# A state-space layer with a gated FFN: parameters turned on VectorE, full-height products first, loads reordered

## The chip, the cores and the metric

The kernel runs on one core of a Trainium2 chip. The time is device microseconds of one launch, the median over several runs; lower is better. Engines: TensorE (PE, matrix products; its weight loads are listed as PEld), VectorE (DVE), ScalarE (ACT), GpSimd (POOL), SyncE (SP, which here only issues DMAs). SP, ACT and POOL each have a queue from which DMAs are issued (SPq, ACTq). "span" is the time from the first to the last instruction in the profile.

## The reference

The input is one sequence of 2048 tokens with 512 features, in bf16. It is normalised, and two branches are multiplied and added to the input:

```python
xn = _layernorm(x, axis=-1)                       # x: 1 x 2048 x 512
s  = _A_ref(xn, ...)                              # linear recurrence over tokens
g  = _silu(_B_ref(xn, w_gate, w_up, w_down))      # gated FFN
return x + s * g

# _A_ref: P = 512 complex states
dt = exp(log_dt);  Lam = Lambda_re + 1j * Lambda_im
Lam_bar = exp(dt * Lam)
B_bar = ((Lam_bar - 1) / Lam)[:, None] * (B_re + 1j * B_im)
Bu = x @ B_bar.T
h[t] = Lam_bar * h[t-1] + Bu[t]
y = 2 * (h @ C.T).real + x * Dskip
# _B_ref: F = 1376
(gelu(x @ w_gate) * (x @ w_up)) @ w_down
```

## The kernel before

The 2048 tokens are cut into NS = 4 stripes of 512 tokens, each of M = 4 tiles of 128 tokens. A stripe goes through these stages:

- **Normalise**: `stats` (VectorE, mean and variance of a tile), `rstd` (VectorE adds epsilon into `ve`, GpSimd raises it to the power -0.5 into `rs`), `norm_dve` (VectorE writes the normalised tile `xn`).
- **Transpose** the tile to `xnT`, features on the partitions. In stripe 0 this is `head_t`: four TensorE transposes into a PSUM bank and a ScalarE eviction (L404). Later stripes use a DMA transpose.
- **Gate and up products** (`gate_pair` in stripe 0, `gate_tile` later): xnT times w_gate and w_up, whose 1376 columns are cut into the chunks `CH` = 512, 512, 352. A ScalarE gelu evicts the one (`gt`), a ScalarE copy the other (`ub`), and VectorE multiplies the two into `at`. Stripe 0 does the first chunk for all four tiles, then the second for all four, then the recurrence's input products, then the last chunk.
- **Recurrence** (`half`): products with B (`BT`), a rotation by tables of sines and cosines (`tab`, made once by `tables` from the angle dt times Lambda_im), a VectorE scan with the real decay `rho` (made by `damping`), and the rotation back into `hst`.
- **Down products** (`down_pair`) with w_down, silu, and **output** (`y_tile`): products of `hst` with C, times silu, plus x, stored.

PSUM holds three double banks (`slots`) and two single ones (`ybank`). A gate chunk of one tile takes one slot; the fourth tile of the first chunk takes the two ybanks. A slot is free for its next products when both evictions are done.

Nothing here runs in the order of the source text. Each piece of work is a step that is added to a plan (class `Plan`) with an engine, a cost in us, what it reads and writes, a lag, and a `rank` that raises its priority. The plan orders the steps on each engine with a list scheduler and a random search over its own modelled times, and emits them in the order of these modelled starts. TensorE's steps alone are chained in the order in which they were added. On the chip each engine works through its own list strictly in order. `not_before` is the earliest modelled start; `after` and `dma_first` chain the first DMAs of a queue.

What the change touches stands at the head of the program:

- `dummies(8, 0)` (L393): eight products of 128x512 on a tile of ones (`warm`, the same memory as `junk`), with which TensorE is kept busy until the first tile arrives. The name `slot<-junk` is theirs.
- `load_p`: three parameter vectors of 512 values (`log_dt`, `Lambda_im`, `Lambda_re`), loaded as four rows of 128 into `pv`.
- `columns` (L674, called by `parameters` and `damping`): turns such rows into columns of four values on 128 partitions, by TensorE products with a 4x4 identity (4 rows of contraction), and a VectorE copy (L676) into `pf`. Before them, exp of log_dt (L356) and the product with Lambda_im (L358) are formed on the rows.
- `spread` (L690): one product with one row of contraction, which broadcasts Dskip to all partitions.
- the two one-element activations at L355 and L357, which bring the exp and the sine table into ScalarE; the third table, gelu, comes with L459.
- the order of the first loads on SP, ACT and POOL.

The order on TensorE before is: dummies, transposes of tile 0, `parameters` (five instructions at L674), one more dummy, gate products of tile 0 (L453), `spread`, transposes of tile 1, up products of tile 0, transposes of tile 2, and so on; `damping`'s product with Lambda_re comes after the second tile.

## Time and profile before

| what | value |
|---|---|
| median of 6 runs | 182.38 us (181.33 to 183.39) |
| the six runs | 183.39, 183.26, 183.27, 181.33, 181.33, 181.49 |
| the profiled execution | 183.39 us, span 181.6 us |
| TensorE busy | 176.3 us, 97% of the span |
| VectorE, ScalarE, GpSimd busy | 157.7, 117.7, 9.7 us |
| granted TensorE clock in the records | 1.00 |
| moved by DMA | 18.01 MB, 99 GB/s on average |

The table is read so: the busy shares are sums over the whole span, and a matrix product counts as busy from its start to its modelled end, overlapping its successor. The time of a launch is longer than the span of the profile by what lies around the first and the last instruction, 1.79 us in the profiled execution. The lines of the profile that carry the argument are shown with the prediction. Line numbers such as L453 are those of the kernel before.

### The profile page before, as it was taken

Reading aid. Unit: us, or ns where it says so; the run is one execution under the profiler, and the core shown is the slowest. Engines: PE = TensorE matmul, PEld = TensorE weight load, DVE = VectorE, ACT = ScalarE, POOL = GpSimd, SP = SyncE. Lnnn points to the kernel's source line nnn. Section 1 sums busy time; section 2 is a strip of 40 time slices with the busy share of each in tenths; the row PEclk is TensorE's granted clock in tenths of the full one; section 3 lists DMA queues with packets and bytes.
Section 4 is the critical chain, followed back from the end, with each engine's and each line's share of the span. In section 5 each row is a group of like instructions: output and inputs, shape, how many; then the busy total and the mean of one; then the engine's idle time right before and its main releaser. Section 6 shows DMA issues by size and latency. Waiting matters only on the chain.

```text
span 181.6 us, 2419 instructions
## 1 busy us (share of the span) xinstructions
PE 176.3 (97%) x856; PEld 84.2 (46%) x856; DVE 157.7 (87%) x267; ACT 117.7 (65%) x179; POOL 9.7 (5%) x21
## 2 busy tenths in 40 slices
PE   6999999999999999999999999999999999999992
PEld 2444444644445554444445544544445554444451
DVE  4859999999999999899999999999999999750063
ACT  5279688899899996866339953726428766454220
POOL 5410220000003000000020000000000000000000
PEclk9999999999999999999999999999999999999999
DMA  5999999995000178440021651451000070720011
GB/s 130 370 304 236 360 116 184 280 210 111 0 0 0 22 145 111 80 79 0 0 87 34 125 115 35 79 110 32 29 0 29 12 142 21 150 85 29 0 58 58
DMA packets 47139, 18.01 MB, mean 99 GB/s; under 512 B 38456, under 2 KB 47128, under 8 KB 47128
## 3 DMA queue, kind: packets, MB, share of 16 engines
q1 hardware_dynamic: 46544, 17.34, 42.3%
q10 hardware_dynamic: 552, 0.53, 1.1%
q8 instruction: 6, 0.10, 0.2%
q14 instruction: 5, 0.04, 0.1%
q0 software_dynamic: 32, 0.00, 0.0%
HBM read 6.33 MB, written 2.10 MB: 46 GB/s over the span
## 4 chain that ended last, share of the span: by engine, by line
PE 96%; DVE 2%; issue 0%; DVEq 0%
PE slot L474 31%; PE slot L517 21%; PE slot L585 15%; PE ybank L547 14%; PE slot L453 10%; PE slot L393 2%; PE ybank L453 1%; PE ybank L401 1%; DVE yg L551 1%; DVE ot L559 1%; PE slot L674 1%; PE slot L690 0%; DVE junk L348 0%; DVE at L352 0%; PE ybank L674 0%
## 5 line engine op out<-in xcount | busy, mean ns | idle before, releaser
L474 PEld LDWEIGHTS <-xnT 128*128 128x128 bf16 x288 | 28.2, 98 | 28.4
L517 PE MATMUL slot<-wd,atT 128*128 128x512 bf16 (+1 forms) x176 | 38.7, 379 | 0.0
L474 PE MATMUL slot<-wu,xnT 128*128 128x512 bf16 (+1 forms) x144 | 31.8, 357 | 0.0
L474 PE MATMUL slot<-wg,xnT 128*128 128x512 bf16 (+1 forms) x144 | 31.8, 357 | 0.0
L618 DVE TENSOR_TENSOR_SCAN Fs<-rho,ini,W 128x512 bf16<-128x512 f32 x24 | 29.2, 1265 | 0.0
L585 PE MATMUL slot<-xnT,BT 128*128 128x512 bf16 x128 | 28.3, 379 | 0.0
L547 PE MATMUL ybank<-C,hst 128*128 128x512 bf16 (+1 forms) x128 | 27.9, 372 | 0.0
L517 PEld LDWEIGHTS <-atT 128*128 128x128 bf16 (+1 forms) x176 | 17.2, 98 | 20.9
L588 ACT ACTIVATE U<-slot 128x1024 bf16<-128x1024 f32 x16 | 16.1, 1019 | 9.2 <-PE slot L585 9.2
L551 DVE TENSOR_TENSOR yg<-ybank,g 128x512 bf16<-128x512 f32 (+1 forms) x14 | 9.4, 669 | 13.7 <-PE ybank L547 13.6
L547 PEld LDWEIGHTS <-hst 128*128 128x128 bf16 x136 | 13.3, 98 | 13.8
L585 PEld LDWEIGHTS <-BT 128*128 128x128 bf16 x128 | 12.5, 98 | 15.0
L599 DVE TENSOR_TENSOR Q<-U,tab 128x4096 bf16<-128x4096 bf16 x8 | 18.3, 2289 | 0.6 <-ACT U L588 0.3
L521 ACT ACTIVATE g<-slot 128x1024 f32<-128x1024 f32 x8 | 8.2, 1023 | 16.3 <-PE slot L517 16.3
L599 DVE TENSOR_TENSOR Q<-Fs,tab 128x4096 bf16<-128x4096 bf16 x8 | 18.3, 2285 | 0.1
L543 ACT ACTIVATE ybank<-sk 128x512 f32<-128x512 bf16 (+1 forms) x14 | 8.2, 585 | 12.8 <-DVE yg L551 11.1
L482 ACT ACTIVATE gt<-slot 128x1024 bf16<-128x1024 f32 x12 | 12.3, 1023 | 4.3 <-PE slot L474 4.2
L482 ACT ACTIVATE ub<-slot 128x1024 bf16<-128x1024 f32 x12 | 12.3, 1023 | 3.4 <-PE slot L474 3.2
L453 PEld LDWEIGHTS <-xnT 128*128 128x128 bf16 x96 | 9.6, 101 | 9.3 <-issue 1.4
L453 PE MATMUL slot<-wg,xnT 128*128 128x512 bf16 (+1 forms) x44 | 11.1, 378 | 0.0
L453 PE MATMUL slot<-wu,xnT 128*128 128x512 bf16 (+1 forms) x44 | 10.7, 366 | 0.0
L776 ACT ACTIVATE junk<-x_tok 128x512 bf16<-128x512 bf16 x16 | 10.0, 627 | 0.3
(120 smaller groups left out, 181.9 us busy)
## 6 DMA issues: line engine op xcount, KB each, us to landing
out_dram<-ot SPq DMA_DIRECT2D x15, 128.0 KB, 1.7
x_tok<-in_A_x_dram SPq DMA_DIRECT2D x3, 512.0 KB, 8.1
wd<-in_B_w_down_dram SPq DMA_DIRECT2D x1, 1280.0 KB
wu<-in_B_w_up_dram SPq DMA_DIRECT2D x2, 512.0 KB, 5.6
x_tok<-in_A_x_dram SPq DMA_DIRECT2D x4, 128.0 KB, 4.1
wg<-in_B_w_gate_dram ACTq DMA_DIRECT2D x1, 512.0 KB, 4.5
wg<-in_B_w_gate_dram SPq DMA_DIRECT2D x1, 512.0 KB
wg<-in_B_w_gate_dram SPq DMA_DIRECT2D x1, 352.0 KB, 4.3
```

Source lines behind the costliest of these rows:

```text
L453: T.matmul(pss[bank][:, 0:w], lhsT=xnT[:, k, t0 : t0 + P], rhs=wt[:, k, a:b], start=(k == 0), stop=(k == KT - 1))
L474: T.matmul(ps[:, bank, 0 : b - a], lhsT=xnT[:, k, t0 : t0 + P], rhs=wt[:, k, a:b], start=(k == 0), stop=(k == KT - 1))
L482: acts(1024, lambda ps=ps, dst=dst, fn=fn: act(out=dst[:, 0:1024].rearrange("p (c w) -> p c w", c=2), in_=ps[:, :, :], func=fn), [("slot", ...
L517: T.matmul(ps[:, b, :], lhsT=atT[:fs, k, m * P : (m + 1) * P], rhs=wd[:fs, k, :], start=(k == 0), stop=(k == NFT - 1))
L521: acts(1024, lambda: act(out=g2[gi][:, :, :], in_=ps[:, :, :], func=AF.Silu), [("slot", i, 0), ("slot", i, 1)], [("g2", gi)], table="silu" ...
L547: T.matmul(bank, lhsT=hst[s % 2][:, j // NPT, j % NPT, m * P : (m + 1) * P], rhs=C2[:, j // NPT, j % NPT, a:z], start=(j == 0 and not seed ...
L551: dve(w, lambda: V.tensor_tensor(out=yg[e][:, a:z], in0=bank, in1=g2[gi][:, b, a:z], op=ALU.mult), [key, ("g2", gi)], [("yg", e, a)], base ...
L585: T.matmul(ps[:, ri, :], lhsT=BT[:, ri, k, pt * P : (pt + 1) * P], rhs=xnT[:, k, (s % 2) * TS : (s % 2 + 1) * TS], start=(k == 0), stop=(k ...
L588: acts(1024, lambda q=q, ps=ps: act(out=U[ui][:, :, q, :], in_=ps[:, :, :], func=AF.Copy), [("slot", i, 0), ("slot", i, 1)], [("U", ui, q)])
L599: dve(4096, lambda: V.tensor_tensor(out=Qf, in0=src.unsqueeze(1).to_broadcast(WQ), in1=table, op=ALU.mult), reads, ["Q"], rate=2.0)
L618: pl.add(DVE, 1.116 if s == 0 else 1.19, lambda ri=ri, q=q, pt=pt, first=first: V.tensor_tensor_scan(out=Fs[:, ri, q, :], data0=rho[:, pt ...
L776: acts(512, lambda i=i, fn=fn, m=m: act(out=junk[:], in_=x_tok[:, s * M + m, :], func=fn, accum_out=sx[:, s, i, m : m + 1]), [("x", s, m)] ...
```

## The change

- **Parameters.** `columns`, `parameters` and the products at L674 are gone. The three vectors are loaded into twelve rows of one 32x128 tile `pv`, which VectorE has cleared before; four VectorE transposes of 32x32 (`turn_rows`) write the columns into `pc`. exp and the product dt times Lambda_im are then done on 128x4 columns. `damping` is added to the plan ahead of the tables.
- **Products before the first gate tile.** Nine and a half dummies in place of eight ahead of the transposes of tile 0, and two of 384 columns in place of one of 512 after them. They read 128 columns of ones, broadcast, so only these are set. `spread` comes after the transposes of tile 1.
- **Loads.** SP issues x tiles 0 and 1, the first chunk of w_gate, x tile 2, the first chunk of w_up, x tile 3, then the second chunks and the rest as before. The first chunk of w_gate was on ScalarE's queue, Dskip on GpSimd's; Dskip is now on ScalarE's.
- **Chunks.** In stripe 0 and in the loads the columns are cut into `CH0` = 384, 512, 480. Later stripes keep `CH`.
- **Ranks.** Tiles 0 and 1 have a raised rank for their statistics and normalising, and so has the first gelu.

```diff
...
+    CH0 = [(0, 384), (384, 896), (896, F)]
...
-    pv = [sb(f"pv{i}", [4, P]) for i in range(3)]
-    pr = [sb(f"pr{i}", [4, P], FP32) for i in range(2)]
+    pv = sb("pv", [32, P])
+    pc = sb("pc", [P, 32])
...
     def load_w(put, eng, q, c, land, which, **kw):
-        a, b = CH[c]
+        a, b = CH0[c]
...
-    def load_p(i, v, land):
-        dma_first(ACT, 0.4, land, lambda: nc.scalar.dma_start(out=pv[i][:], in_=v.rearrange("(k p) -> k p", p=P)), [("pv", i)], not_before=0.72)
+    def load_p(i, v):
...
+        dma_first(ACT, 0.4, 1.8, lambda: nc.scalar.dma_start(out=pv[4 * i : 4 * i + 4, :], in_=v.rearrange("(k p) -> k p", p=P)),
+            [("pv", i)], not_before=0.72)
...
     def load_x(eng, q, m, land):
...
-    load_p(0, A_log_dt, 2.0)
-    load_p(1, A_Lambda_im, 2.0)
-    load_w(dma_first, ACT, nc.scalar, 0, (0.47, 4.4), 0)
-    behind = [first[ACT]]
-    dma(ACT, 0.4, 4.6, lambda: nc.scalar.dma_start(out=pv[2][:], in_=A_Lambda_re.rearrange("(k p) -> k p", p=P)), writes=[("pv", 2)], after=behind, rank=-20.0)
-    for m in range(M):
-        load_x(SP, nc.sync, m, (1.75, 1.9, 2.8, 3.0)[m])
-    for c, which, land in ((0, 1, 3.7), (1, 0, 3.9), (1, 1, 3.9)):
-        load_w(dma_first, SP, nc.sync, c, (1.45, land), which)
+    dve(32, lambda: V.memset(pv[:], 0.0), writes=[("pv", i) for i in range(3)], not_before=0.72, rank=450.0)
+    load_p(0, A_log_dt)
+    load_p(1, A_Lambda_im)
+    load_p(2, A_Lambda_re)
+    dma(ACT, 0.4, 3.0, lambda: nc.scalar.dma_start(out=Drow[0:1, :], in_=A_Dskip.rearrange("(a d) -> a d", a=1)), writes=["Drow"], after=[first[ACT]], rank=-20.0)
+    def load_first(c, which, land):
+        load_w(dma_first, SP, nc.sync, c, (1.45 * (CH0[c][1] - CH0[c][0]) / 512, land), which)
...
+    load_x(SP, nc.sync, 0, 1.75)
+    load_x(SP, nc.sync, 1, 1.9)
+    load_first(0, 0, 2.1)
+    load_x(SP, nc.sync, 2, 2.1)
+    load_first(0, 1, 2.2)
+    load_x(SP, nc.sync, 3, 2.2)
+    load_first(1, 0, 2.6)
+    load_first(1, 1, 2.8)
...
-        load_w(dma_first, SP, nc.sync, 2, (1.0, 4.1), which)
+        load_w(dma_first, SP, nc.sync, 2, (1.35, 4.1), which)
...
-    id4 = sb("id4", [4, 4], FP32)
...
-    dma(POOL, 0.7, 3.4, lambda: G.dma_start(out=Drow[0:1, :], in_=A_Dskip.rearrange("(a d) -> a d", a=1)), writes=["Drow"], rank=200.0, not_before=1.2)
-    pool(0.25, lambda: G.tensor_copy(out=id4[:], in_=ident[0:4, 0:4]), ["ident"], ["id4"], rank=190.0)
...
-    dve(480, lambda: V.memset(warm[:], 1.0), writes=["warm", "junk"], not_before=0.6, rank=300.0)
...
+    dve(64, lambda: V.memset(warm[:, 0:P], 1.0), writes=["warm", "junk"], not_before=0.72, rank=400.0)
...
-    acts(1, lambda: act(out=tiny[:], in_=zero[:], func=AF.Exp), ["zero"], ["tiny"], table="exp", rank=150.0, after=behind)
-    acts(128, lambda: act(out=pr[0][:], in_=pv[0][:], func=AF.Exp), [("pv", 0), "tiny"], ["dtr"], table="exp", rank=150.0)
-    acts(1, lambda: act(out=tiny[:], in_=zero[:], func=AF.Sin), ["zero", "dtr"], ["tiny"], table="silu", rank=150.0)
-    dve(128, lambda: V.tensor_tensor(out=pr[1][:], in0=pv[1][:], in1=pr[0][:], op=ALU.mult), [("pv", 1), "dtr"], ["thr"], base=0.13)
...
+    acts(1, lambda: act(out=tiny[:], in_=zero[:], func=AF.Exp), ["zero"], ["tiny"], table="exp", rank=150.0, after=[first[ACT]])
+    pf = small("pf", 8)
+    dt_, thn = pf[:, 0:4], pf[:, 4:8]
+    lim, lre = pc[:, 4:8], pc[:, 8:12]
...
+    def turn_rows():
+        for b in range(4):
+            V.transpose(out=pc[32 * b : 32 * b + 32, :], in_=pv[:, 32 * b : 32 * b + 32])
...
+    pl.add(DVE, 0.3, turn_rows, [("pv", i) for i in range(3)], ["ldt", "lim", "lre"], lag=0.13, rank=50.0)
+    acts(4, lambda: act(out=dt_, in_=pc[:, 0:4], func=AF.Exp), ["ldt", "tiny"], ["dt"], table="exp", rank=150.0)
+    acts(1, lambda: act(out=tiny[:], in_=zero[:], func=AF.Sin), ["zero", "dt"], ["tiny"], table="silu", rank=150.0)
+    dve(4, lambda: V.tensor_tensor(out=thn, in0=lim, in1=dt_, op=ALU.mult), ["lim", "dt"], ["thn"])
...
+    def urgent(s, m):
+        return (60.0, 30.0, 0.0, 0.0)[m] if s == 0 else 0.0
...
     def stats(s, m):
...
-        dve(512, f, [("x", s, m)], [("st", s, m)], base=0.12)
-        dve(6, lambda: V.bn_aggr(out=mv[:, s, m, :], in_=st[:, s, m, :]), [("st", s, m)], [("mv", s, m)], base=0.08)
+        rank = urgent(s, m)
+        dve(512, f, [("x", s, m)], [("st", s, m)], base=0.12, rank=rank)
+        dve(6, lambda: V.bn_aggr(out=mv[:, s, m, :], in_=st[:, s, m, :]), [("st", s, m)], [("mv", s, m)], base=0.08, rank=rank)
...
     def rstd(s, a, b):
...
-            [("mv", s, m) for m in range(a, b)], [("ve", s, m) for m in range(a, b)])
+            [("mv", s, m) for m in range(a, b)], [("ve", s, m) for m in range(a, b)], rank=urgent(s, a))
...
-    def dummies(k, i):
+    def dummies(k, i, n=KT):
...
-                T.matmul(slots[i][:, 0, :], lhsT=warm[:, 0:P], rhs=warm[:], start=True, stop=True)
-        pl.add(PE, k * 0.427, f, ["warm", "junk"], [("slot", i, 0)], lag=0.22)
+                T.matmul(slots[i][:, 0, 0 : n * P], lhsT=warm[:, 0:P], rhs=warm[:, 0:P].unsqueeze(1).to_broadcast([P, n, P]), start=True, stop=True)
+        pl.add(PE, k * 0.107 * n, f, ["warm", "junk"], [("slot", i, 0)], lag=0.22)
...
-    pf = small("pf", 16)
-    lim, dt_, thn, lre = (pf[:, 4 * i : 4 * i + 4] for i in range(4))
...
     def norm_dve(s, m):
...
-            op0=ALU.subtract, op1=ALU.mult), [("x", s, m), ("mv", s, m), ("rs", s, m)], [("xn", m)], rate=2.0)
+            op0=ALU.subtract, op1=ALU.mult), [("x", s, m), ("mv", s, m), ("rs", s, m)], [("xn", m)], rate=2.0, rank=urgent(s, m))
...
-        a, b = CH[c]
+        a, b = CH0[c]
...
-        acts(w, lambda: act(out=gd, in_=pss[0][:, 0:w], func=AF.Gelu_apprx_tanh), both, [("gt", q)], table="gelu", after=early if c == 0 else ())
+        acts(w, lambda: act(out=gd, in_=pss[0][:, 0:w], func=AF.Gelu_apprx_tanh), both, [("gt", q)], table="gelu", after=early if c == 0 else (), rank=40.0 if c + m == 0 else 0.0)
...
-                pe(KT, 512, mm(ps, c, wt, c), [("xnT", s % 2, m), (nm, c)], [("slot", i, c)])
+                pe(KT, 512, mm(ps, c, wt, c), [("xnT", s % 2, m)] + [(nm, n) for n in range(3)], [("slot", i, c)])
...
-            pe(KT, b - a, mm(ps, kind, wt, 2), [("xnT", s % 2, m), (nm, 2)], [("slot", i, kind)])
+            pe(KT, b - a, mm(ps, kind, wt, 2), [("xnT", s % 2, m)] + [(nm, n) for n in range(3)], [("slot", i, kind)])
...
-    def columns(rows, ps, key, o, writes):
...
-        def f():
-            for i, (src, idn, _) in enumerate(rows):
-                T.matmul(ps[:, 4 * i : 4 * i + 4], lhsT=src[:], rhs=idn, start=(i == 0), stop=(i == len(rows) - 1))
-        pe(len(rows), 150, f, [r[2] for r in rows] + ["ident", "id4"], [key])
-        dve(4 * len(rows), lambda: V.tensor_copy(out=pf[:, o : o + 4 * len(rows)], in_=ps[:, 0 : 4 * len(rows)]), [key], writes, base=0.14)
...
-    def parameters():
-        columns(((pv[1], ident[0:4, 0:4], ("pv", 1)), (pr[0], id4[:], "dtr"), (pr[1], id4[:], "thr")), slots[1][:, 0, 0:12], ("slot", 1, 0), 0, ["lim", "dt", "thn"])
...
     def damping():
-        columns(((pv[2], ident[0:4, 0:4], ("pv", 2)),), ybank[0][:, 0:4], ("y", 0), 12, ["lre"])
...
-    dummies(8, 0)
+    dummies(9, 0)
+    dummies(1, 0, 2)
...
     head_t(0)
-    parameters()
-    dummies(1, 0)
+    dummies(2, 0, 3)
+    damping()
     tables()
-    then = {0: ((spread, lambda: head_t(1)), (lambda: head_t(2),)), 1: ((), (lambda: head_t(3),))}
+    then = {0: ((lambda: head_t(1), spread), ()), 1: ((lambda: head_t(2),), (lambda: head_t(3),))}
...
-        if m == 1:
-            damping()
...
```

## The prediction, made before the changed kernel ran

> **What bounds the kernel now.** I read the busy shares first, then the list of waits on TensorE, then the chain that ended last in order of time, and last the timeline of the first 17 us.
>
> ```profile
> PE 176.3 (97%) x856; PEld 84.2 (46%) x856; DVE 157.7 (87%) x267; ACT 117.7 (65%) x179; POOL 9.7 (5%) x21
> PE slot L393 <- DVE at L352: 1.7, 1, 1.7
> ```
>
> The second line is the whole list of TensorE's waits: it waits once, 1.7 us before its first product, and then never. From 1.66 to 176.28 us it is one unbroken queue, and a 5.3 us tail of VectorE and the last store follows. So the time is what stands in that queue, and how fast the array runs. An edit on another engine counts only if it shortens the queue's head or tears a hole in it. The head, from the chain (start, us, what):
>
> ```profile
> 1.66 3.60 PE slot L393 x8
> 5.26 0.61 PE ybank L401 x4
> 5.87 0.97 PE slot L674 x5
> 6.84 0.54 PE slot L393
> 7.38 1.71 PE slot L453 x4
> 9.09 0.54 PE slot L690
> 9.62 0.54 PE ybank L401 x4
> 10.16 1.25 PE slot L453 x4
> 11.40 0.22 PE ybank L401 x4
> 11.63 1.73 PE slot L453 x8
> 13.58 0.11 PE ybank L674
> ```
>
> Four 512-column products take 1.71 us at 7.38 and eight take 1.73 at 11.63: 0.43 against 0.216 us each. The array runs at half speed until about 10.8 us (the group at 10.16 is the mixed one). The granted-clock row reads 9 all along and does not show it; the durations do. Between 7.38 and 11.40 four groups took 1.71 + 0.54 + 0.54 + 1.25 = 4.04 us; at full speed they are 0.86 + 0.23 + 0.22 + 0.86 = 2.18. **Half speed costs 1.86 us of real work**, and the five narrow products at L674 cost 0.97 more, plus a filler.
>
> ```profile
> 2.99 0.69 DVE L378 BATCH_NORM_STATS2 st<-x_tok 128x6 f32<-128x512 bf16 x1 [1.37 <-DMA x_tok<-in_A_x_dram]
> 4.18 0.58 POOL L383 TENSOR_TENSOR rs<-ve,mhalf 128x1 f32<-128x1 f32 x1 [1.16 <-DVE ve L386]
> 4.80 0.41 DVE L420 TENSOR_SCALAR xn<-x_tok,mv,rs 128x512 bf16<-128x512 bf16 x1
> 5.91 0.60 ACT L404 ACTIVATE xnT<-ybank 128x512 bf16<-128x512 bf16 x1 [0.64 <-PE ybank L401]
> 14.49 1.28 ACT L459 ACT_TABLE_LOAD   x1
> 15.79 1.57 ACT L459 ACTIVATE gt<-slot 128x512 bf16<-128x512 f32 x3
> ```
>
> These show what the first gate tile needs: x lands at 2.99, statistics, power, normalised tile at 5.21, transposed, evicted by 6.51. The gate tile starts at 7.38, so 0.87 us of the narrow products and filler stand after its data are there.
>
> **The sum, part by part**, against the profiled execution: 183.39 us, of which 181.6 are the span and 1.79 lie around it.
>
> *First gate tile.* x tile 0 is still SP's first issue, so 5.21 for the normalised tile stands. The transposes start at 5.26; cold, their eviction starts 0.65 later (5.91); at full speed 0.26 later (as 11.40 to 11.66 further on). Add 0.60 for the eviction and 0.06 for the signal: 6.2 to 6.6. The two new 384-column fillers take 0.64 cold, 0.32 warm, inside the eviction. I take 6.2 and 0.25 for ScalarE being late (see its part below): **6.45, that is -0.93**.
>
> *Clock.* VectorE clears 32x128 and 128x128 elements before TensorE may begin, instead of the whole list up to the 128x512 (0.48 us, 1.11 to 1.60). By share of that row this is about 0.25, from 0.81: fillers from about 1.15. Nine and a half of them at 0.43 last 4.06 us, to 5.2, where the transposes follow; nothing narrow comes before the gate tile. So TensorE is filled with full-height products from 1.15 on. The Trainium skill (TensorE: Matmul & The Clock Gate, "The HAM clock gate") says that full rate comes after about 3.4 us of sustained work, judged in free-running windows of that length, so between 3.4 and 6.8 us after the start. The row first: before began at 1.66 and was fast only at 10.8, 9.1 us later. By the rule alone that should be 5.1 to 8.5, and the edit would be worth little. Counted from 6.84, where the narrow products end, the rule gives 10.2 to 13.7, which holds 10.8. That makes the narrow products the likely break. After the change it gives 4.5 to 8.0. I take the gate work at full speed: **-1.86**. At 8.0 it would lose (8.0 - 6.45) / 2 = 0.8. The same section speaks against banking all this: the moment is run-variable and not to be fitted. The six runs do fall in two groups, 181.33 to 181.49 and 183.26 to 183.39; the profile is one of the slow group, and the fast group may have 1.9 us of this already.
>
> *Lambda_re's own product* at 13.58 leaves the queue: **-0.10**. Gate columns 384 + 512 + 480 are still 1376 in the same number of products: 0.
>
> *VectorE turns the rows.* Four 32x32 transposes; no such row. The nearest are the 128x4 operations at L727 to L734, eight in 0.67 us, so four in about 0.38; the two copies at L676 (0.17 and 0.16) and L358 (0.26) go. The turn waits for three tiny loads, the first of which now waits for the clearing (issue about 0.95 in place of 0.73); the third is issued at about 1.86. The first load landed within 2.73 us (issued 0.73, read at 3.46), and the tile of x took 2.25; I take 2.25, so 4.1. Behind the turn on VectorE's queue stand the second tile's statistics (0.69) and the normalising of tile 0, whose power ends at 4.76. From 4.09 the gap is 0.67, the two together 1.07: from 0 to 0.4 on the path; tile 0 has the highest rank, so 0.
>
> *ScalarE.* Exp moves behind the turn: 4.1 + 0.38 + 0.1, then 0.2; the sine table (1.28 + 0.20) would hold ScalarE from about 4.8 to 6.3, where the eviction of tile 0 wants to start at 5.5 to 5.9. Before it was over at 5.27. If loads land earlier or the order is swapped: 0; as priced: up to 0.8; I take 0.25 (in the 6.45). Here a second rule differs: the skill (ScalarE: Activation LUTs, "What ACT_TABLE_LOAD costs") adds a drain of 1.38 to the 1.28. The row shows the load at 14.49 and the first gelu at 15.79, with the operation before it ending at 14.47: no drain. By the rule the gate tile would come up to 1.4 later still (181.9); the row decides.
>
> *Loads.* SP now issues x0, x1, wg, x2, wu, x3, then the second chunk; the first wg leaves ScalarE's queue, and Drow moves there from POOL's, behind the three rows (about 2.1 against 2.29). The one-us windows carry 763 KB to 5 us and 370 to 380 KB in each us after. In this order wg is complete after 640 KB (about 4.7), x2 at 5.0, wu at 6.1, x3 at 6.4, the second chunk at 9.3. Needed: wg 6.45, wu 7.6, second chunk about 12.7. Cover of 1.5 us and more: 0. The later issues (x block, BT, last chunk, wd) keep their order and number, and half-steps need BT at about 20, wg's last chunk at 27: 0. *Rho* is now formed early: a 1.13 us power on POOL, in the way of a later tile's 0.58 if placed ahead; 0 to 0.5, taken 0 because tiles 2 and 3 have 1 us in hand.
>
> Sum: 183.39 - 0.93 - 1.86 - 0.10 = **180.5**. That is 1.0% under the median of 182.38, 1.6% under the slow group, 0.5% under the fast one. One per cent is about what a measurement of this kernel can tell from no change.
>
> **Rivals.** *ScalarE becomes the bound at the fourth chunk of products.* The first chunk is now 4 x 1.3 + 0.9 + 0.2 = 6.3 us, so the second wants its bank at 12.7; that bank needs the first gelu. Before, gelu ran at 15.79 for a bank wanted at 17.08. ScalarE has from 6.45: four evictions and broadcasts (2.4), sines (0.82), table (1.28), up, gelu (0.9): 5.4 of 6.3 us, and 1.1 more with sp, cp and one more up-tile. For it: it also idled 3.69 us before 10.20, waiting. A hole of 0.7 gives 181.2.
>
> *The clock stays cold to 10.8* whatever stood in the queue: (10.8 - 6.45) / 2 = 2.2 more, 182.7. For it: the broadcast at 9.09 has one row and did not stop the clock. Against: the 0.97 us lie in the last window before.
>
> *Slower: the tiny loads hold tile 0.* VectorE works in order. If the turn stands ahead of the normalising and the third load takes 4.4 us, as Drow's 1 KB did from POOL's queue, it lands at 6.3, the turn ends at 6.65, tile 0 at 7.06 and not 5.21: 1.85 later. TensorE then has run out of fillers at 5.2, idles 1.9 us, and starts cold again: 1.85 + 1.86 on top, 184.2 and a little more for a later landing. It is slower than 182.38 from 1.9 us of the two together. Against: 2.73 is the ceiling seen for such a load on ScalarE's queue.
>
> **Chances.** Forecast (180.0 to 181.0) 0.58; ScalarE's hole (181.0 to 182.3) 0.18; cold clock 0.09; tiny loads 0.15. Of the forecast and the little that may lie below it, and counting a before that falls into its slow group, 0.48 end more than 1% faster; 0.37 within 1%; 0.15 slower. The range leaves out only the last: 179.9 to 182.8.
>
> **What would show it.** Right: TensorE's first product near 1.15; no L674 kind of product; L453's first products at 0.16 us each, from 6.3 to 6.7; no TensorE wait after the first; the second chunk near 12.7; the last product near 173.4. Wrong: first gate products of 0.32 us (clock), a wait of TensorE on gelu's tile at 12 to 14 us (ScalarE), statistics or normalising of tile 0 released by the row loads (tiny loads), any DMA as the releaser of L453.

## The result, and the profile after

The changed kernel takes **183.79 us** (median of 36 runs, 181.99 to 185.72); the kernel before, run beside it on the same chip, takes 181.56 (73 runs, 180.99 to 184.74). The forecast was 180.5, the range 179.9 to 182.8. The medians differ by 1.2%. The ratio is **1.0061, 95% from 1.0036 to 1.0087**; it leaves out every run more than 1.5% above its kernel's fastest, which drops 10 of the changed kernel's 36 runs, so here the medians and the groups say more. Ratios below are made the same way, against the kernel before run beside the experiment, with the 95% interval behind them.

The times come in groups. Spans of the changed kernel (the profiled run counted in): 12 of 37 runs from 180.2 to 180.9 us, 15 from 181.5 to 182.5, 10 from 183.1 to 183.9. Spans of before, over the four comparisons of this study (252 runs): 145 at or below 180.2, 97 between 180.2 and 182, 10 above. The profile of before (span 181.6) is of its middle group, the profile of after (182.29 us, span 180.5) of its lowest. Laid side by side, the two profiles make the change look 1.1 us faster. Group against group it is slower, by the groups' medians 180.45 against 179.5 in the lowest, 182.0 against 181.4 and 183.55 against 182.8 in the two above, and it falls into its upper groups more often (25 of 37 against 107 of 252). Both halves of this have to be explained.

From the page of the changed kernel, the busy shares; then the whole list of TensorE's waits in the trace (engine, tile and line, what released it, us in total, times, longest). A hole below is time in which TensorE stands idle.

```profile
PE 174.1 (96%) x853; PEld 82.9 (46%) x853; DVE 157.8 (87%) x270; ACT 118.0 (65%) x179; POOL 9.0 (5%) x19
```

```profile
PE slot L413 <- DVE zero L357: 1.1, 1, 1.1
PE ybank L421 <- DVE xn L438: 1.1, 1, 1.1
PE slot L471 <- ACT xnT L424: 0.5, 1, 0.5
PE slot L471 <- ACT gt L477: 0.2, 1, 0.2
```

Before, this list had one line. Now TensorE waits three more times: 1.1 us for the normalised tile 0, 0.5 for its eviction, and once on the first gelu. The same in the timeline of TensorE in the changed kernel (start, us, what, [idle before it <- releaser]):

```profile
1.11 4.23 PE L413 MATMUL slot<-junk 128*128 128x512 bf16 x10 [1.11 <-DVE zero L357]
6.45 0.40 PE L421 MATMUL ybank<-ident,xn 128*128 128x128 bf16 x4 [1.10 <-DVE xn L438]
6.68 0.49 PE L413 MATMUL slot<-junk 128*128 128x384 bf16 x2
7.64 0.82 PE L471 MATMUL slot<-wg,xnT 128*128 128x384 bf16 x4 [0.47 <-ACT xnT L424]
...
13.29 0.81 PE L471 MATMUL ybank<-wu,xnT 128*128 128x384 bf16 x4
14.34 1.02 PE L471 MATMUL slot<-wg,xnT 128*128 128x512 bf16 x4 [0.23 <-ACT gt L477]
```

The fillers end at 5.34. Tile 0 comes at 6.45, its gate products at 7.64, where 6.45 was forecast and before had 7.38. In this run the array is at full speed from 6.45 on (0.82 us for four 384-column products), so the forecast's clock term is there. The second chunk starts at 14.34; the products before it are issued to 13.94 (13.29 + 4 x 0.16), so 0.40 is lost in front of it (the list counts from their modelled ends and shows 0.2).

Why tile 0 is late is in VectorE's timeline of the changed kernel:

```profile
3.81 0.15 DVE L406 TENSOR_SCALAR ve<-mv 128x1 f32<-128x1 f32 x1
4.50 0.85 DVE L369 STREAM_TRANSPOSE pc<-pv 32x32 bf16<-32x32 bf16 x4 [0.54 <-DMA pv<-in_A_Lambda_re_dram]
5.38 0.69 DVE L397 BATCH_NORM_STATS2 st<-x_tok 128x6 f32<-128x512 bf16 x1
5.99 0.40 DVE L438 TENSOR_SCALAR xn<-x_tok,mv,rs 128x512 bf16<-128x512 bf16 x1
```

VectorE is done with tile 0's variance at 3.96 and then takes the turn, which waits for the third row. GpSimd's power for tile 0 runs meanwhile (4.04, 0.57 us) and is done at 4.61; tile 0 could be normalised then. It is normalised at 5.99: the rest of the turn and the statistics of tile 1 stand in front of it, 1.38 us. And from the chain that ended last, in order of time, how ScalarE passes it on:

```profile
1.83 2.54 DMA pv<-in_A_Lambda_re_dram
...
5.61 1.28 ACT L373
6.90 0.20 ACT tiny L373
7.10 0.49 ACT xnT L424
7.64 0.82 PE slot L471 x4
...
8.69 0.32 PE slot L696
...
11.54 0.60 ACT xnT L424
12.14 0.35 ACT cbt L663
12.51 1.28 ACT L477
13.80 0.50 ACT gt L477
```

The sine table (L373) keeps ScalarE until 7.10, where the transposes would have let the eviction start at about 6.7 (6.45 + 0.26). The end of this stretch is a second chain of ScalarE: eviction of tile 3, cosine, gelu's table, first gelu, and only then the bank for the second chunk.

The profiled pair adds up: gate tile +0.26, clock -1.86, the broadcast of D and the narrower first tile +0.27, Lambda_re's product -0.10, the hole +0.40. That is -1.03, and the start of the last group of products before the tail does move from 170.92 to 169.88. (The +0.27: in the chain the broadcast L696 takes 0.32, not 0.22, and the first four 384-column products 0.82, not 0.65.)

### The profile page after: what moved, and what is told of

It is laid out like the page before. It is cut to its first block, busy times and chain, and to the rows that moved or that the text cites. A ratio compares the mean times of both kernels' runs of the same rounds, so it can differ in the third digit from the quotient of the medians.

```text
span 180.5 us, 2411 instructions
## 1 busy us (share of the span) xinstructions
PE 174.1 (96%) x853; PEld 82.9 (46%) x853; DVE 157.8 (87%) x270; ACT 118.0 (65%) x179; POOL 9.0 (5%) x19
## 4 chain that ended last, share of the span: by engine, by line
PE 90%; ACT 3%; DMA 2%; DVE 2%; issue 0%; ACTq 0%; DVEq 0%
PE slot L492 31%; PE slot L535 21%; PE slot L603 15%; PE ybank L565 13%; PE slot L471 9%; DMA pv<-in_A_Lambda_re_dram 1%; DMA out_dram<-ot 1%; DVE ot L577 1%; ACT L477 1%; ACT L373 1%; ACT xnT L424 1%; DVE yg L569 1%; DVE pc L369 0%; PE ybank L421 0%; ACTq L319 0%
## 5 line engine op out<-in xcount | busy, mean ns | idle before, releaser
L492 PEld LDWEIGHTS <-xnT 128*128 128x128 bf16 x288 | 28.2, 98 | 28.4
L492 PE MATMUL slot<-wg,xnT 128*128 128x512 bf16 (+1 forms) x144 | 31.8, 357 | 0.0
L492 PE MATMUL slot<-wu,xnT 128*128 128x512 bf16 (+1 forms) x144 | 31.8, 357 | 0.0
L565 PEld LDWEIGHTS <-hst 128*128 128x128 bf16 x136 | 13.3, 98 | 13.8
L471 PEld LDWEIGHTS <-xnT 128*128 128x128 bf16 x96 | 9.1, 98 | 10.1 <-ACT xnT L424 0.9
L471 PE MATMUL slot<-wg,xnT 128*128 128x512 bf16 (+2 forms) x44 | 10.4, 360 | 0.7 <-ACT xnT L424 0.5
L781 ACT ACTIVATE junk<-x_tok 128x512 bf16<-128x512 bf16 x16 | 10.1, 629 | 0.8 <-DMA x_tok<-in_A_x_dram 0.6
L471 PE MATMUL slot<-wu,xnT 128*128 128x512 bf16 (+2 forms) x44 | 10.5, 360 | 0.0
```

Of the source, the lines that this page charges most:

```text
L471: T.matmul(pss[bank][:, 0:w], lhsT=xnT[:, k, t0 : t0 + P], rhs=wt[:, k, a:b], start=(k == 0), stop=(k == KT - 1))
L492: T.matmul(ps[:, bank, 0 : b - a], lhsT=xnT[:, k, t0 : t0 + P], rhs=wt[:, k, a:b], start=(k == 0), stop=(k == KT - 1))
L565: T.matmul(bank, lhsT=hst[s % 2][:, j // NPT, j % NPT, m * P : (m + 1) * P], rhs=C2[:, j // NPT, j % NPT, a:z], start=(j == 0 and not seed ...
L781: acts(512, lambda i=i, fn=fn, m=m: act(out=junk[:], in_=x_tok[:, s * M + m, :], func=fn, accum_out=sx[:, s, i, m : m + 1]), [("x", s, m)] ...
```

## The experiments

Two theories were on the table after this profile. **Late tile:** the turn stands on VectorE's queue ahead of tile 0; that costs a fixed stretch at the head, and the holes it tears keep the array at half speed for one or two more stretches in some runs, which makes the groups. **ScalarE:** the sine table, or ScalarE's work as a whole, is what is late. A third question is about before: are its narrow products what keeps its clock low?

The order on each engine comes from the planner. Where an experiment says "X behind Y", a planned start was raised, with what depends on it, before the orders were written out, and nothing else (i is to stand behind j):

```
-        start = best[1]
+        start = list(best[1])
+        for i, j in self.later:
+            start[i] = max(start[i], start[j] + 1e-6)
...
```

### The changed kernel again

No edit; a second profile, meant to catch an upper group.

> The changed kernel once more, as the measure for the others on the same chip. Its runs so far fall in three groups, near 182.2, 183.8 and 185.4 us, 1.6 apart. Theory A (the clock): the groups differ by how many windows of about 3.4 us the array stays at half speed after tile 0, so a profile that falls in an upper group shows gate products of 0.32 us in place of 0.16 for one or two times 3.4 us, and nothing else late. Rival B (a late load or another wait): the profile of an upper group shows a wait of TensorE in place of slow products.

Measured 183.87 (six runs, 183.44 to 184.96; ratio 1.0115, 1.0062 to 1.0168). The profiled run took 183.44. TensorE's timeline:

```profile
6.44 0.61 PE L421 MATMUL ybank<-ident,xn 128*128 128x128 bf16 x4 [1.10 <-DVE xn L438]
...
7.74 1.46 PE L471 MATMUL slot<-wg,xnT 128*128 128x384 bf16 x4
...
10.10 0.82 PE L471 MATMUL slot<-wu,xnT 128*128 128x384 bf16 x4
...
15.50 1.02 PE L471 MATMUL slot<-wg,xnT 128*128 128x512 bf16 x3 [0.23 <-ACT gt L477]
```

The transposes start at the same time as before (6.44 against 6.45), but take 0.61, and the first gate products 1.46. The array is at half speed to about 10 us and the second chunk comes 1.16 later. TensorE's list of waits has no new line: between these two runs the difference is the clock. This profile is of the middle group; none of the highest was caught, and that it lost two stretches is read from its distance alone. The Trainium skill (TensorE: Matmul & The Clock Gate, "The HAM clock gate") has the rate decided once in a free-running window of about 3.4 us; one more window at half speed is 1.7 us of lost work by that (an estimate), and the middles of the groups here lie 1.55 apart (180.45, 182.0, 183.55). Rule and runs agree.

### More fillers, same orders

```
-    dummies(9, 0)
+    dummies(9, 0, more=3)
...
-    dummies(2, 0, 3)
+    dummies(2, 0, 3, more=3)
```

> The order of every engine is that of the changed kernel; only three more products of 512 columns stand before the transposes of tile 0 and three more of 384 after them, so that TensorE does not idle between 5.3 and 7.6 us. Theory A (the holes of 1.1 and 0.5 us leave a window unfilled, and the clock stays down for another one): the lowest group stays near 182.2, the upper groups go or shrink, the median falls from 183.8 to about 182.5. Rival (the groups come from where the window happens to lie, and holes of this size do not matter): the same three groups in the same shares, median 183.8 or, by the products in the way, up to 0.7 more.

Measured 182.81 (22 runs; ratio 1.0053, 1.0026 to 1.0080). All spans lie between 180.5 and 181.1: the two upper groups are gone. So the **holes make the upper groups**, and they are worth 1.0 us of the median. What is left over before's 181.49 on this chip, 1.3 us, is there in every run; the next experiment takes 1.1 of it away. The profiled run (span 181.0) shows the rows at work. Its third row load took 3.07 us (1.83 to 4.90) and not 2.54:

```profile
5.03 0.85 DVE L369 STREAM_TRANSPOSE pc<-pv 32x32 bf16<-32x32 bf16 x4 [1.14 <-DMA pv<-in_A_Lambda_re_dram]
```

```profile
6.97 0.40 PE L421 MATMUL ybank<-ident,xn 128*128 128x128 bf16 x4 [1.64 <-DVE xn L438]
...
14.87 1.02 PE L471 MATMUL slot<-wg,xnT 128*128 128x512 bf16 x3 [0.23 <-ACT gt L477]
```

The turn starts 0.53 later than in the first profile of the changed kernel, and the second chunk stands 0.53 later too (14.87 against 14.34). Both runs are at full speed from tile 0 on, so the whole of this delay reaches the second chunk. (In this run the clock rose while the fillers ran, so they were over early and TensorE idled 1.64 us all the same; it stayed at full speed.)

### The turn behind tile 0

```
+    pl.later = [(turned_rows, n0), (exp_dt, e0)]
```

n0 is the normalising of tile 0, e0 the eviction of its transposes. The sine table follows exp.

> The four VectorE transposes of the parameter rows stand behind the normalising of tile 0 in place of ahead of the statistics of tile 1, and exp and the sine table behind the eviction of tile 0; nothing else moves. Theory (the wait for the rows, 4.40 us, and the 0.85 us of the turn hold tile 0): tile 0 is normalised from about 4.7 and not 6.0, the first gate product starts near 6.4 in place of 7.64, the fillers reach the transposes without a hole, and every group falls by about 1.2, less what gelu then comes late (up to 0.8). Rival (tile 0 is held by something else, its load or its power): the first gate product stays at 7.6 and the time does not move.

Measured **181.69** (22 runs, 181.40 to 182.12; ratio 0.9978, 0.9952 to 1.0004), one group only. TensorE's timeline:

```profile
5.17 0.40 PE L426 MATMUL ybank<-ident,xn 128*128 128x128 bf16 x4 [0.50 <-DVE xn L443]
5.41 0.49 PE L418 MATMUL slot<-junk 128*128 128x384 bf16 x2
6.26 0.82 PE L476 MATMUL slot<-wg,xnT 128*128 128x384 bf16 x4 [0.36 <-ACT xnT L429]
7.45 0.40 PE L426 MATMUL ybank<-ident,xn 128*128 128x128 bf16 x4 [0.36 <-DVE xn L443]
...
13.50 1.02 PE L476 MATMUL slot<-wg,xnT 128*128 128x512 bf16 x3 [0.23 <-ACT gt L482]
```

The place of four instructions on one queue, with exp and the sine table that depend on them, is worth 2.1 us of the median (the sine table alone is not it, as the next run shows). The gate tile is at 6.26, even before the forecast 6.45. But of the 1.38 us won there, only 0.84 reaches the second chunk (14.34 to 13.50): tile 1 now waits 0.36 for VectorE, which turns rows when it should work on tile 1, and the hole before the second chunk stays.

### Only the sine table moved

```
+    pl.later = [(sine, e0)]
```

> Only the sine table's load moves, behind the eviction of tile 0. Theory: ScalarE is free when the transposes of tile 0 end (about 6.75), so the first gate product starts at about 7.35, 0.3 earlier than in the changed kernel; but gelu's table comes no earlier, so the hole before the second chunk grows by as much and the time stays within 0.3. Rival (ScalarE's sine load is what costs the 1.2 us at the head): the gate tile starts at 6.4 or so.

Measured 183.64 (22 runs; ratio 1.0040, 1.0004 to 1.0075), spans in the same three groups (10, 5 and 7 of 22). In its profile, one of the middle group, the eviction of tile 0 waits for TensorE alone; but the third row load took 2.83 us, tile 0 came at 6.73, and the gate tile started at 8.03 where 7.35 was expected. The theory that the sine table alone is the delay falls.

### Is it the narrow products, or the late start, that costs before its clock?

Three edits of the kernel with the turn behind tile 0, each giving back to it something that before has: the narrow products in place of the two fillers behind tile 0; the later start (an extra clearing first, fillers from 1.66 in place of 1.11, one filler less); and both. `narrow=True` stands for one bf16 and two float32 products of 4 rows.

```
-    dummies(2, 0, 3)
+    dummies(2, 0, 3, narrow=True)
```

```
-    dve(64, lambda: V.memset(warm[:, 0:P], 1.0), ...
+    dve(64, lambda: (V.memset(hst[0][:, 0, 0, :], 1.0), V.memset(warm[:, 0:P], 1.0)), ...
```

> The kernel with the turned rows behind tile 0 (all its runs in one group, 181.4 to 182.1), with one edit: in place of the two fillers of 384 columns after the transposes of tile 0 stand products of the form that the kernel before had there, one 4x128 bf16 and two 4x128 float32 with four columns (about 0.97 us). They add nothing to the result. Theory N (the narrow products break the window): a part of the runs, as large as the upper groups of the kernel before (about 45 of 100), goes up by 1.5 or more, and a profile of such a run has slow gate products; the lowest group lies about 0.3 higher. Rival (the narrow products cost only the time they take): one group, 0.2 to 0.5 higher.

> The kernel with the turned rows behind tile 0, with one edit: VectorE fills another 128x512 tile before the tile of ones, so that TensorE's fillers start at about 1.6 and not 1.1 us, as in the kernel before; one filler less. Theory S (the start of the fillers, not the narrow products, decides which window is filled): upper groups return, in about 45 of 100 runs, 1.5 us or more higher. Rival N (narrow products decide): one group as before the edit, within 0.2 us.

> The kernel with the turn behind tile 0, with both edits that alone made hardly an upper group: the fillers start at 1.66 with one filler less, and narrow products (0.6 to 1 us) stand in place of the two fillers after tile 0, as in the kernel before. Theory (a window of some 3.4 us must be filled to about three quarters, and only windows that begin late enough after the start of the fillers and end early enough in the narrow products are): the start cuts one side, the narrow products the other, so 3 to 5 runs in 10 lie 1.2 us or more above the lowest group, as in the kernel before. Rival (the upper group of the kernel before has another cause): at most 3 of 22, as with either edit alone.

Narrow alone: 181.80, 3 of 22 spans at 181.1 to 181.2, the others to 180.5 (ratio 0.9978, 0.9951 to 1.0005). Late alone: 181.98, one spread from 179.6 to 180.8 (0.9965, 0.9939 to 0.9990). Both: 182.06, **6 of 14** at 181.2 to 181.5 and 8 at 179.7 to 180.1 (1.0032, 0.9993 to 1.0070). Together the two bring back the split of before (107 of 252 above its lowest group). The counts are small: 6 of 14 stands clear of the late start alone (0 of 22), but from narrow products alone (3 of 22) only if the two other kernels with narrow products and an early start, further down, are counted with it (3 of 22 each). The forecast's reading "the narrow products are the likely break" was half the cause at most. With three times the narrow products:

> As the kernel with narrow products in place of the two fillers after tile 0 (3 of 22 runs went up by 1.3), but each narrow product three times: the array sees about 1.8 us of them in place of 0.6. They add nothing to the result. Theory (a window of about 3.4 us counts as filled when some three quarters of it are; narrow products count as nothing): with 1.8 us, more than half of a window, most windows that touch them fail, so half of the runs or more lie 1.5 to 2 us above the others, and the gate products of such a run take 0.32 us. The lowest group lies 1.0 to 1.3 higher, since the gate tile waits for the narrow products. Rival (narrow products only take their time): one group, 1.0 to 1.3 higher.

Measured 182.97 (22 runs; ratio 1.0039, 1.0010 to 1.0068), 13 spans from 179.8 to 180.5, 6 from 181.3 to 181.7, 3 from 183.6 to 183.8. The profile caught one of the last:

```profile
5.76 0.99 PE L423 MATMUL slot<-nf 4*128 4x4 f32 x4
...
8.44 1.46 PE L484 MATMUL slot<-wg,xnT 128*128 128x384 bf16 x4
...
12.04 1.49 PE L484 MATMUL slot<-wg,xnT 128*128 128x384 bf16 x4
13.32 0.44 PE L434 MATMUL ybank<-ident,xn 128*128 128x128 bf16 x4
```

TensorE has no wait from its first product to the second chunk and still runs at half speed to 13.3. Narrow products count little towards the clock. The lowest group barely moved for the extra narrow products (expected was 1.0 to 1.3 more). The holes behind them, 0.36 for tile 1 and 0.40 before the second chunk, could have taken them up; no profile of that group was taken, so this is not shown.

### Closing the hole of tile 1, and the one before the second chunk

```
+    pl.later = [(turned_rows, n0), (turned_rows, v_1), (exp_dt, e0), (s_2, n1), (thn_, n1)]
```

The turn behind tile 1's variance too, and tile 1 normalised before the statistics of tile 2; then the same with the first chunk at 512 columns again, planned anew.

> As the kernel with the turned rows behind tile 0, but with the turn also behind the statistics of tile 1, and tile 1 normalised before the statistics of tile 2. Theory: the hole of 0.36 us before the transposes of tile 1 closes (start 6.9 to 7.1 and not 7.45) and the time falls by 0.3, if gelu for the second chunk does not give it back. Rival (the hole before the second chunk takes all that the head gains, since the sine table and the angles follow the turn): the second chunk starts at 13.5 as before, no change.

> As e2_ve1, with the first chunk back at 512 columns (the planner orders anew; the turn stays where e2_ve1 has it). The first chunk's four tiles then last 1.7 us longer, with the same total of columns. Theory: gelu of tile 0 is ready before its bank is wanted again, the hole of 0.40 us before the second chunk goes, and the time falls by 0.4 against e2_ve1, to 180.9 to 181.1, below the lowest group of the kernel before. Rival (the hole moves to another wait, or the anew ordered plan loses elsewhere): no gain against e2_ve1, or a wait of TensorE of 0.4 or more at another place.

Measured 181.79 (22 runs; ratio 0.9982, 0.9957 to 1.0007) and 181.84 (0.9990, 0.9964 to 1.0016). In the first, tile 1's transposes come at 6.96 in place of 7.45, tile 2's then wait 0.24, and the second chunk stands at 13.61: nothing won. In the second there is no hole before the second chunk, but the profiled run, the slowest of its 22, has these in TensorE's list of waits:

```profile
PE slot L542 <- ACT U L613: 0.7, 1, 0.7
PE ybank L428 <- DVE xn L445: 0.3, 1, 0.3
PE slot L478 <- ACT xnT L431: 0.3, 1, 0.3
PE slot L499 <- ACT gt L507: 0.3, 1, 0.3
```

In these two traces, what is won at the head is taken back by VectorE or ScalarE behind it.

### The order of the loads

The kernel with the turn behind tile 0, and SP's first eight issues in the order of before (four x tiles, then weights).

> The kernel with the turn behind tile 0, in which only SP's order is taken back: the four tiles of x first, then the first chunks of w_gate and w_up; every other order stays. Theory (the loads were covered and gave nothing): within 0.2 us of 181.7, and no wait of TensorE on a load. Rival (tiles 2 and 3 were early by the old order, or w_gate late): with x first VectorE does not wait for tile 2 or 3 and the second chunk starts 0.2 to 0.4 earlier, or the first gate tile waits for w_gate beyond 6.3.

Measured 181.61 (22 runs; ratio 0.9991, 0.9965 to 1.0017), second chunk at 13.47 against 13.50. The gate tile waits 0.2 for wg and starts at 6.62, and that is gone by the second chunk. In this kernel the order of the loads is worth nothing at the end.

### The parameters another way

Back on TensorE as in before (planned anew); or loaded straight into columns by the DMA, with no turn at all:

```
-    ... nc.scalar.dma_start(out=pv[4 * i : 4 * i + 4, :], in_=v.rearrange("(k p) -> k p", p=P)) ...
+    ... nc.scalar.dma_start(out=pc[:, 4 * i : 4 * i + 4], in_=v.rearrange("(k p) -> p k", p=P)) ...
```

> The changed kernel with one part undone: the parameters are turned into columns by TensorE's narrow products as before, behind the transposes of tile 0, with a filler of 256 columns after them; earlier and more fillers, order of the loads, chunk of 384 and ranks stay as changed; the planner orders anew. Theory (the turn on VectorE is what the change loses by): tile 0 is normalised near 4.8, the first gate product starts at 6.5 to 7.2 and not 7.64, and the median falls from 183.8 to 181.3 to 182.0. Rival (loads, chunk or ranks lose as well): it stays above 182.5.

> The kernel with the turn behind tile 0, but no turn at all: each parameter vector is loaded straight as four columns on 128 partitions (512 elements of two bytes, strided), and VectorE neither clears nor transposes. Theory (VectorE is the bound of the head, so 0.85 us taken off it counts): the transposes of tile 1 start near 6.9 and not 7.45, the sine follows 0.5 to 0.8 earlier, the second chunk starts at 12.9 to 13.2 and not 13.5, and the median falls by 0.3 to 0.6, to about 181.2. Rival (the many two-byte descriptors land late or hold up the loads of x): the columns land after 6 us, exp and the sine come later than in the kernel with the turn, and it is slower than 181.7.

On TensorE: 182.49 (22 runs; ratio 1.0037, 1.0008 to 1.0066), 0.5 above what was expected; 3 of its spans are at 182.1 to 182.2. The head is better than that of any kernel with the turn on VectorE: tile 0 normalised at 4.72, gate tile at 6.49, second chunk at 13.18 with no gelu wait, 0.32 ahead of the kernel with the turn behind tile 0. Then TensorE waits for ScalarE after all (from its list of waits):

```profile
PE slot L486 <- ACT gt L494: 0.3, 1, 0.3
PE slot L465 <- ACT U L600: 0.2, 1, 0.2
```

The products behind these waits, U's first, start at 28.96 and 97.31; in the kernel with the turn behind tile 0 the same products start at 28.93 and 96.77. So the wait for U costs the 0.32 and a little more, the wait for the gelu another 0.51, and the last group before the tail starts at 169.58 against 169.04. The new order that the planner found loses at these two places. As columns: 181.94 (14 runs; ratio 1.0002, 0.9970 to 1.0033), second chunk at 14.04 where 12.9 to 13.2 was expected. The three issues take 0.47 to 0.53 us each of ScalarE's queue (those of rows 0.55, 0.26 and 0.32), and x arrives later, as VectorE's timeline shows:

```profile
3.15 0.69 DVE L401 BATCH_NORM_STATS2 st<-x_tok 128x6 f32<-128x512 bf16 x1 [2.02 <-DMA x_tok<-in_A_x_dram]
...
6.72 0.69 DVE L401 BATCH_NORM_STATS2 st<-x_tok 128x6 f32<-128x512 bf16 x1 [1.08 <-DMA x_tok<-in_A_x_dram]
```

### The kernel before with nothing but earlier and more fillers

```
-    dve(480, lambda: V.memset(warm[:], 1.0), ...
+    pl.front = dve(480, lambda: V.memset(warm[:, 0:P], 1.0), ...     # first on VectorE's queue
...
-    dummies(8, 0)
+    dummies(8, 0, more=2)
```

> The kernel before with one edit: VectorE sets the tile of ones first and only its 128 columns, so TensorE's fillers start near 1.05 in place of 1.66, and there are ten of them in place of eight. The parameters stay on TensorE, loads and chunks as before. Theory (filled windows): the first gate product and the lowest group stay (181.1 to 181.4), and the upper groups of the kernel before (4 to 5 runs in 10, near 183.2) shrink to 1 or 2 in 10; the median falls to 181.3. Rival (the narrow products alone make the groups): shares as before, about 45 of 100 above 182.5.

Measured **181.37** (22 runs, 180.98 to 183.46; ratio 0.9991, 0.9962 to 1.0021), the lowest median of all. 19 of 22 spans are at 179.2 to 179.8 and 3 at 181.4 to 181.5; of before on that chip 42 of 67 were in the low group. The ratio cannot tell it from before; what it seems to change is how often the upper group comes, and 3 of 22 against 25 of 67 is not enough to prove that. TensorE's timeline:

```profile
1.05 3.95 PE L395 MATMUL slot<-junk 128*128 128x512 bf16 x10 [1.05 <-DVE zero L352]
5.19 0.40 PE L403 MATMUL ybank<-ident,xn 128*128 128x128 bf16 x4 [0.18 <-DVE xn L422]
...
6.29 1.03 PE L455 MATMUL slot<-wg,xnT 128*128 128x512 bf16 x4
...
14.65 1.03 PE L455 MATMUL slot<-wg,xnT 128*128 128x512 bf16 x4
```

The gate tile is at 6.29 with the narrow products still in front. The second chunk at 14.65 corresponds to 12.92 with 384 columns (eight groups of four products, each 0.866 instead of 0.65), so it is 0.58 ahead of the kernel with the turn behind tile 0. That is about the 0.5 between the two spans, 179.2 and 179.7.

Last, the same with the rows turned as bf16 on TensorE and exp on the columns, planned anew:

> The kernel before with the early fillers (median 181.37, 3 of 22 runs 2 us above), and with its narrow products cut down: the three parameter vectors are turned by one bf16 product each, and exp and the product with dt are done on columns as in the changed kernel; no float32 product of four rows is left. The planner orders anew. Theory: the narrow products take 0.2 us in place of 0.6 to 1.0, the upper group goes, the lowest group stays at 181.0 to 181.4, since the eviction of tile 0 (6.2) starts the gate tile already; the median is 181.2. Rival (exp and the sine table then come behind tile 0, gelu comes late for the second chunk, and the time rises by 0.5 or more): the second chunk starts after 15.0 and TensorE waits for gelu.

Measured 183.94 (22 runs; ratio 1.0039, 1.0002 to 1.0076), spans from 180.3 to 183.9 in three groups. Neither expectation had the reason. VectorE's timeline and one line of TensorE's:

```profile
5.49 0.69 DVE L376 BATCH_NORM_STATS2 st<-x_tok 128x6 f32<-128x512 bf16 x1 [0.89 <-DMA x_tok<-in_A_x_dram]
6.10 0.40 DVE L418 TENSOR_SCALAR xn<-x_tok,mv,rs 128x512 bf16<-128x512 bf16 x1
```

```profile
6.55 0.40 PE L399 MATMUL ybank<-ident,xn 128*128 128x128 bf16 x4 [1.46 <-DVE xn L418]
```

The planner put the statistics of tile 2 ahead of normalising tile 0; they waited for x, tile 0 was late by as much as in the changed kernel, and the same three groups came. No turn on VectorE is in this kernel. It is the mechanism a second time, from another cause: an instruction with a late input ahead of tile 0 on VectorE's queue.

## Why the prediction was wrong, step by step

**First gate tile, -0.93: wrong, and the step that failed.** It is the term of VectorE turning the rows: "from 0 to 0.4 on the path; tile 0 has the highest rank, so 0." Tile 0 waited 1.38 us for it and for the statistics behind it. Three things in it were off.

- The row loads: the third one was read at 4.37 (1.83 + 2.54) against 4.1.
- The turn: 0.85 us, 0.20 for each 32x32 block, against 0.38. The estimate came from operations of 128x4, of which eight overlap into 0.67 us; these four do not overlap.
- The place: a rank chooses among steps whose inputs are ready or nearly so. In the plan that the kernel's own code works out, the power of tile 0 runs from 4.08 to 4.73. The turn fills that gap at 3.96, on rows that the plan has landing 1.8 us after issue and with a cost of 0.30; the statistics of tile 1 follow to 4.91, and tile 0 is normalised then. On the chip the turn starts 0.54 later and lasts 0.55 longer, the queue keeps its order, and tile 0 is normalised at 5.99.

Moving those four instructions back, with exp and the sine table, is worth 2.1 us. The 0.25 for ScalarE was near in size (the eviction starts at 7.10 where the transposes would allow some 6.7), but it hides under other waits: with the sine table moved alone the median falls by 0.15, which is within the groups' scatter.

**Clock, -1.86: right in the profiled run, but not a gain to bank.** In the profiled run the gate work is at full speed and the term is in the sum. But before's lowest group, 6 runs in 10, very likely has it already: it lies 1.9 us under the next, although no profile of it was taken. The text said so and the number did not take it in. And the late tile leaves TensorE empty from 5.34 to 6.45 and from 7.17 to 7.64, which puts two runs of three into the upper groups. "TensorE is filled from 1.15 on" was the condition, and it was not met. The reason given for before was half right at most: the split came back in full only with the late start and the narrow products together.

How full must a window be? From single profiles, with the 3.4 us of the Trainium skill's section named above, an estimate: windows were lost with 1.1 us idle in them (the changed kernel's second profile), with 0.97 of narrow products (before, 4.0 to 7.4 if its windows end where the speed changes) and with about 0.9 of them (three times the narrow products, 3.2 to 6.6 by the same count). So 70 to 75% of full-height products was not enough there. No run measured the limit itself.

**Lambda_re's product, -0.10, the loads, 0, and rho, 0:** as forecast; rho's power runs at 13.27, behind those of all four tiles. Of the parts of the change, the raised ranks are the one that no run took back.

**The sum.** From the forecast 180.43 to the profiled 182.29 it is 1.19 for the gate tile (7.64 against 6.45), 0.40 for the hole before the second chunk, and the 0.27 named above, by which the sum overstated what full speed gives. From there to the median, 1.5 us, it is the groups: the median run is one of the middle group.

**Rival one, ScalarE's hole before the second chunk:** true, beside the main error: 0.40 in the changed kernel, 0.39 in its second profile, still there with the turn behind tile 0. Even with the turn repaired, the change lands at 181.69, not at 180.5: 13.50 for the second chunk against about 12.7 forecast is the larger part.

**Rival "the clock stays cold to 10.8" whatever stands in the queue:** not as stated, since the first profile is at full speed from 6.45. In the second, half speed lasts to 10.1.

**Rival "tiny loads hold tile 0":** the right mechanism at 0.15. It was sized on a load landing at 6.3, and set aside because "2.73 is the ceiling" for one on ScalarE's queue. The load that did the harm took 2.54, and two other profiles show 2.83 and 3.07, so it is no ceiling; the slower turn and the tile behind it were enough. Its 184.2 lies near the 183.79 measured partly by luck: it has tile 0 at 7.06 and the whole clock term lost, where tile 0 came at 5.99 and the groups lose none, one or perhaps two stretches.

## What to carry to other kernels

Before an instruction with a late input goes on an in-order queue, list what stands behind it and ask what happens if the input comes half a microsecond late. A planner's rank does not protect the urgent work, since it acts only once that work is ready, or nearly so, in the plan. In this head VectorE was short of time and TensorE had some to spare, so the work was moved the wrong way. And a single profile belongs to one group of runs; two profiles compared without their groups can show the sign wrong, as here. Where a start-up clock is at stake, count how many of twenty runs fall in each group. Here the cheapest edit, earlier and more fillers, had the lowest median of all, though not clear of before: it is the one to try first.

## What the runs showed of the hardware that was not expected

- A 32x32 transpose on VectorE takes 0.20 us, and four in a row 0.85: they do not overlap, while eight operations of 128x4 took 0.67 in before.
- Busy is not enough for the clock: where three rounds of products of 4 rows by 4 columns stood behind tile 0, one run kept TensorE without a wait and at half speed to 13.3 us, and 9 of 22 spans lay above the lowest group. With full-height fillers in the same place all 22 spans lie in one group, and the profiled run is at full speed from tile 0 on.
- The granted-clock row does not show this: over the first 10 us it reads 9 in every slice, in the profile of after at full speed and in that of its second run at half speed alike. The durations of equal products do (0.82 against 1.46 us).
- The same 1 KB load of a parameter row took 2.54, 2.56, 2.83 and 3.07 us in four profiles in which VectorE waited for it. Once the array was warm, the half microsecond between the first and the last reached the second chunk whole (14.34 and 14.87).
- A load of columns with two bytes each cost 0.47 to 0.53 us of the issuing queue. The third x tile of 128 KB then came late: VectorE waited 1.08 us and took it up at 6.72, against 5.61 in the kernel with the same order of loads and rows for TensorE.
